# A grouped-query decode step with a gated MLP: 64 rows of an MLP weight in five groups, x in the result's layout by products, and nine scratch products per head

## The chip, the cores and the metric

The kernel runs on one core of a Trainium2 chip. The core has a matrix engine (TensorE, PE in the rows; PEld is its loading of the stationary operand), a vector engine (VectorE, DVE), a scalar engine (ScalarE, ACT), GpSimd (POOL) and SyncE (SP), which here only issues transfers. Sixteen DMA engines move data between HBM and the core's memory. The metric is the device time of one launch in microseconds (us), as a median over runs; lower is better.

## The reference, cut to what matters

One decode step for eight sequences of width 512, all in float32: a normalised x goes through attention over a cache of 4096 keys and values (32 query heads, 8 key/value heads of width 128), and through a gated MLP whose result, after a silu, multiplies the attention's result; x is added at the end.

```python
def _A_ref(x, k_cache, v_cache, wq, wo):
    q = (x @ wq).reshape(B, 1, 32, 128).transpose(0, 2, 1, 3)
    k, v = repeat(k_cache, 4, axis=1), repeat(v_cache, 4, axis=1)
    p = softmax(einsum("bhqd,bhkd->bhqk", q, k) * 128 ** -0.5)
    return einsum("bhqk,bhkd->bhqd", p, v).reshape(B, 1, 4096) @ wo

def _B_ref(x, w_in, w_sp, b_sp, w_out):
    z = gelu(x @ w_in)                         # 512 -> 1792
    z1, z2 = z[..., :896], layernorm(z[..., 896:])
    return (z1 * (w_sp * z2 + b_sp)) @ w_out   # 896 -> 512

xn = layernorm(x)
return x + _A_ref(xn, ...) * silu(_B_ref(xn, ...))
```

## The kernel before

**Data and slots.** The caches are 268 MB, and nearly all of the rest of the traffic is wq, wo and the MLP's weights. Three slots in the core's memory, a, b and c, take 8.39 MB each (128 partitions of 64 KB). A key/value head needs four slot loads: two halves of K (four sequences each) and two halves of V. SyncE issues all loads from one queue in a fixed order (`loads`): for each head the second half of K into b, the first half of V into c, the second half of V into b, and then the next head's first half of K into a. Before each it waits on a counter that TensorE raises (`pe`, eight steps a head), so that a load starts only when the slot's last reader is done; it stands one or two loads ahead of TensorE. After the last V come six pieces of wo into slot a (`WO_PIECES`, of 36, 16, 4, 4, 3 and 1 half-columns), and last x in the result's layout (`x_rows`, 128 rows of 256 bytes).

**The prologue** (`prologue`) runs under a scheduler that orders work by its dependencies. It loads wq into b, x (8 rows) and the MLP's weights (`w_mlp`, 128 rows) into c, and the first half of K into a. It normalises x, makes all q (L150), and when wq has been read, issues the next half of K into b (L160). Then it computes the MLP: z (L175), gelu, layernorm, the transposes to `hT` (L205), the product with `w_out` in seven blocks of 128 rows (L210, which writes four 32-row groups of one bank side by side), a re-layout by a selection matrix `pick` (L216) and the gate. Only then may slot c be loaded with V.

**A head** (`head_products` on TensorE, a hardware loop of eight turns, and `head_sides` on the other engines): 64 score products (L353), a softmax whose maxima and sums go across partitions by three small products (L357 to L361), the transpose of p, 32 products with each half of V (L372), and a fold of the output (L382), before whose second half two scratch products run (L379). Each take of a semaphore (`take`, L341) stands in TensorE's queue ahead of the products that need it. The second half of V is a separate wait.

**The end** (`last_products`, `last_sides`): for wo's rows of the first seven heads, 56 products in two accumulators (L408), which wait piece by piece; then the last head's rows directly (L417), the two accumulators copied out (one by VectorE, one by ScalarE) and folded in by `pick` (L430), and the last two rows of wo (L417 again). VectorE multiplies by the gate and adds x (both shown as L258), and ScalarE issues the store.

Of the kernel before, what the change touches and what calls it, by code (L numbers as in the profile page):

```python
# [10 lines left out]
P = 128  # L11
B, D = 8, 512
HKV, REP, S, DH = 8, 4, 4096, 128
NK = D // P
G = 4
J = S // (G * P)
R = 32
FH = 896
FQ = 256
NB = FH // P  # L20
# [5 lines left out]
W = 64  # L26
OUT_ROWS = 2 * B
# [1 line left out]
FOLDED = HKV * REP - REP  # L29
AHEAD = FOLDED + 2  # L30
HD = 256
N_IN, N_OUT = NK * 2 * FH, NB * D
N_MLP = N_IN + N_OUT + R
STEPS = 8
WARM = 384


class Chip:
# [49 lines left out]
        self.same_all = self.same.rearrange("p g r -> p (g r)")  # L88


def prologue(tc, t, x, w_mlp, wq, k0, k1, landed_a, landed_b):

    nc = tc.nc
    slot_a, slot_b, slot_c = t.slots
    nc.sync.dma_start(slot_b, wq)
    wq_sb = slot_b.rearrange("p (k n) -> p k n", k=NK)
    w_in_sb = slot_c[:, :N_IN].rearrange("p (k n) -> p k n", k=NK)
    w_out_sb = slot_c[:, N_IN:N_IN + N_OUT].rearrange("p (j d) -> p j d", j=NB)
    side_sb = slot_c[:, N_IN + N_OUT:N_MLP]
    x_sb = slot_c[:B, N_MLP + P:N_MLP + P + D]  # L100
    xn = slot_c[:B, N_MLP + P + D:N_MLP + P + 2 * D]
    nc.sync.dma_start(x_sb, x)
    nc.sync.dma_start(slot_c[:, :N_MLP], w_mlp)
    first = nc.sync.dma_start(slot_a, k0).then_inc(landed_a, 16)
    tc.no_tile_sem_insts.add(first.ins.name)

# [21 lines left out]
    def scratch(*shape):  # L128
        turn[0] ^= 1
        n = 1  # L130
        for s in shape[1:]:
            n *= s
        return t.scr[turn[0]][:shape[0], :n]
# [11 lines left out]
    for quad in range(HKV // G):  # L145
        pq = scratch(P, REP * DH)
        for k in range(NK):
            for g in range(G):
                lo = (quad * G + g) * REP * DH
                nc.tensor.matmul(pq[R * g:R * (g + 1), :], t.xnT[:, k, :], wq_sb[:, k, lo:lo + REP * DH],  # L150
                                 start=(k == 0), stop=(k == NK - 1))
# [12 lines left out]
    z, u_sb = zu[:, 0], zu[:, 1]  # L164
    rest = t.pT.rearrange("p j b g r -> p (j b g r)")
    hT, y_sb = rest[:, :2 * P].rearrange("p (a s) -> p a s", a=2), rest[:, D:]
# [36 lines left out]
    for a in range(2):  # L203
        th = scratch(P, P)
        nc.tensor.transpose(th, u_sb[:, 1, a * P:(a + 1) * P], t.ident)  # L205
        nc.vector.tensor_copy(hT[:, a, :], th)
    pw = scratch(P, D)
    for j in range(NB):
        g, a = divmod(j, 2)
        nc.tensor.matmul(pw[R * g:R * (g + 1), :], hT[:, a, R * g:R * (g + 1)], w_out_sb[:, j, :],  # L210
                         start=(a == 0), stop=(a == 1 or j == NB - 1))
    nc.vector.tensor_copy(y_sb, pw)
    py = scratch(P, W)
    for g in range(G):
# [6 lines left out]
    nc.vector.tensor_scalar(e, e, 1.0, None, op0=ALU.add)  # L221
    nc.vector.reciprocal(e, e)
    nc.vector.tensor_mul(t.gate, py, e)


def place_q(nc, t, h):
# [3 lines left out]
class Heads:  # L230
# [2 lines left out]

    def __init__(self, nc, t, landed_a, landed_b, stored):
        self.nc, self.t = nc, t
        self.pe, self.dve, self.act = (nc.alloc_semaphore(s) for s in ("pe", "dve", "act"))
        self.token, self.part1 = nc.alloc_semaphore("token"), nc.alloc_semaphore("part1")
        self.landed_a, self.landed_b, self.landed_c = landed_a, landed_b, nc.alloc_semaphore("landed_c")  # L240
        self.landed_wo = [nc.alloc_semaphore(f"landed_wo{i}") for i in range(len(WO_PIECES))]
        self.landed_x = nc.alloc_semaphore("landed_x")
        self.stored = stored
        self.nv = self.na = 0
        self.end = HKV * STEPS
        half_d = D // 2
        self.part = [t.sc[:, 0, :half_d], t.o_ps[0].rearrange("p g d -> p (g d)")[:, :half_d]]
# [13 lines left out]
    def tell(self):  # L261
        self.nc.vector.wait_ge(self.dve, self.nv).then_inc(self.token, 1)

    def loads(self, kT, v, wo, x_rows):
        sync, (a, b, c) = self.nc.sync, self.t.slots
        for h in range(HKV):
            at = h * STEPS
            if h:
                sync.wait_ge(self.pe, at - 8 + 7)
                sync.dma_start(b, kT[h, 1]).then_inc(self.landed_b, 16)  # L270
                sync.wait_ge(self.pe, at - 8 + 6)
            sync.dma_start(c, v[h, 0]).then_inc(self.landed_c, 16)
            sync.wait_ge(self.pe, at + 2)
            sync.dma_start(b, v[h, 1]).then_inc(self.landed_b, 16)
            sync.wait_ge(self.pe, at + 1)
            if h < HKV - 1:
                sync.dma_start(a, kT[h + 1, 0]).then_inc(self.landed_a, 16)
        for (lo, hi), landed in zip(WO_PIECES, self.landed_wo):
            sync.dma_start(a[:, lo * HD:hi * HD], wo[:, lo * HD:hi * HD]).then_inc(landed, 16)
        sync.dma_start(self.t.x_out, x_rows).then_inc(self.landed_x, 16)  # L280

    def head_sides(self, h):

# [41 lines left out]
    def last_sides(self, out):  # L325
        nc, t, vec = self.nc, self.t, self.nc.vector
        self.v(vec.tensor_copy, t.part_sb[0], self.part[0], pe=self.end + 1)
        self.tell()
        nc.scalar.wait_ge(self.pe, self.end + 2)
        nc.scalar.copy(t.part_sb[1], self.part[1]).then_inc(self.part1, 1)  # L330
        vec.wait_ge(self.act, self.na).then_inc(self.act, -self.na)
        self.v(vec.tensor_mul, t.gate, t.acc, t.gate, pe=self.end + 3)
        vec.wait_ge(self.landed_x, 16).then_inc(self.landed_x, -16)
        self.v(vec.tensor_add, t.gate, t.gate, t.x_out, own=True)
        nc.scalar.wait_ge(self.dve, self.nv)
        nc.scalar.dma_start(out, t.gate).then_inc(self.stored, 16)
        nc.scalar.wait_ge(self.dve, self.nv).then_inc(self.dve, -self.nv)
        vec.wait_ge(self.pe, self.end + 3).then_inc(self.pe, -(self.end + 3))
# [4 lines left out]
    def head_products(self):  # L343
        nc, t, step = self.nc, self.t, lambda mm: mm.then_inc(self.pe, 1)
        slot_a, slot_b, slot_c = t.slots
        for half, (slot, landed) in enumerate(((slot_a, self.landed_a), (slot_b, self.landed_b))):
            self.take(landed, 16)
            k_sb = slot.rearrange("p (i c g s) -> p i c g s", i=HALF, c=2, g=G)
            for i in range(HALF):
                b = half * HALF + i  # L350
                for c in range(2):
                    for g in range(G):
                        mm = nc.tensor.matmul(t.sc[R * g:R * (g + 1), c, :], t.q[:, b * R:(b + 1) * R],  # L353
                                              k_sb[:, i, c, g, :], start=(b == 0), stop=(b == B - 1))
            step(mm)
        self.take(self.token, 1)
        step(nc.tensor.transpose(t.scr[0][:1, :P], t.nm, t.ident))  # L357
        self.take(self.token, 1)
        step(nc.tensor.transpose(t.scr[1][:, :1], t.full.rearrange("b g r -> b (g r)"), t.ident[:1, :1]))
        self.take(self.token, 1)  # L360
        step(nc.tensor.matmul(t.scr[1][:, 1:2], t.same_all, t.wl, start=True, stop=True))  # L361
        self.take(self.token, 1)
        pT = t.pT.rearrange("p j b g r -> p j b (g r)")
        for half, (slot, landed) in enumerate(((slot_c, self.landed_c), (slot_b, self.landed_b))):
            if half:
                self.take(self.token, 1)
            self.take(landed, 16)
            v_sb = slot.rearrange("p (i j e) -> p i j e", i=HALF, j=J)
            of = t.o_ps[half].rearrange("p g d -> p (g d)")
            for j in range(J):  # L370
                for i in range(HALF):
                    mm = nc.tensor.matmul(of[R * i:R * i + G * REP, :], pT[:, j, half * HALF + i],  # L372
                                          v_sb[:, i, j], start=(j == 0), stop=(j == J - 1))
            step(mm)
        n = HALF * REP
        for half in range(2):
            if half:
                for _ in range(2):
                    nc.tensor.matmul(t.scr[1][:, :WARM], t.ident, pT.rearrange("p j b x -> p (j b x)")[:, :WARM],  # L379
                                     start=True, stop=True)  # L380
            self.take(self.token, 1)
            mm = nc.tensor.matmul(t.po[:, half * n:(half + 1) * n], t.o_sb[half],  # L382
                                  t.fold.rearrange("p i r -> p (i r)"), start=True, stop=True)
        step(mm)
# [53 lines left out]
        step(mm)  # L438


def gqa_gmlp_decode(nc, x, kT, v, wq, wo, w_mlp, x_rows, out):
    t = Chip(nc)
    landed_a, landed_b, stored = (nc.alloc_semaphore(s) for s in ("landed_a", "landed_b", "stored"))
    with tile.TileContext(nc) as tc:
        prologue(tc, t, x, w_mlp, wq, kT[0, 0], kT[0, 1], landed_a, landed_b)
    heads = Heads(nc, t, landed_a, landed_b, stored)
    heads.loads(kT, v, wo, x_rows)
    for h in range(HKV):
        heads.head_sides(h)
    heads.last_sides(out)  # L450
    nc.sync.wait_ge(stored, 16).then_inc(stored, -16)
    with nc.tensor.Fori(0, HKV):
        heads.head_products()
    heads.last_products()
# [39 lines left out]
```

## Time and profile before

| | |
|---|---|
| median of 3 runs | 678.75 us (678.70 to 679.01) |
| the profiled execution's own time | 679.39 us |
| its span, first to last instruction | 678.1 us |
| TensorE busy | 351.0 us (52%) |
| VectorE busy | 80.7 us (12%) |
| 16 DMA engines, SyncE's queue | 99.1% of the span |
| HBM read | 290.78 MB, 429 GB/s over the span |
| TensorE's granted clock, mean | 0.748 |

The page's second part cuts the span into 40 slices and gives each engine's busy share in tenths; its third part gives what each DMA queue moved. A timeline gives single instructions, or runs of the same, in order of time, with the idle time ahead of them in brackets and what ended it. "PEq" is TensorE's own queue: an instruction stood there for a semaphore. A DMA row gives the size and the time from issue to landing. The granted clock is given as a share of 2.4 GHz, so 0.50 is 1.2 GHz.

### The profile page before, as it was taken

The page shows a single profiled execution, that of the slowest core. Times are in us where ns is not written, and L with a number is a line of the kernel's source. Part 1 is how long each engine was busy: PE and PEld are TensorE (multiplying, and loading weights), DVE is VectorE, ACT ScalarE, POOL GpSimd, SP SyncE. Part 2 cuts the span into 40 slices and gives each one's busy share as a digit, 9 for nine tenths or more (in the row PEclk, how much of TensorE's full clock was granted, in tenths as well). Part 3 has the DMA queues.
Part 4 walks back from the last instruction along what each step waited for, and adds up shares of the span by engine and source line. Part 5 has one row for each costly group of instructions (what it writes and reads, how often), then busy time and mean ns, then how long its engine had stood idle before and what let it go on. Part 6 is the DMA issues. An engine that isn't in the chain of part 4 may idle for free. (4 is left out here: it accounts for less than half of the span.)

```text
span 678.1 us, 5431 instructions
## 1 busy us (share of the span) xinstructions
PE 351.0 (52%) x2480; PEld 102.7 (15%) x2480; DVE 80.7 (12%) x156; ACT 13.8 (2%) x28; POOL 2.8 (0%) x15
## 2 busy tenths in 40 slices
PE   0446743545565444456555444655645454655548
PEld 0112210111121111111111110111111111211104
DVE  0142021102110021101100021101101021100111
ACT  0010000000000000000000000000000000000000
POOL 1000000000000000000000000000000000000000
PEclk9986766778767677877766677887666678877659
DMA  9999999999999999999999999999999999999996
GB/s 383 439 433 434 434 433 433 434 433 433 433 433 433 433 433 433 437 437 437 445 437 433 437 437 433 441 437 433 433 433 433 433 433 433 433 433 433 433 414 287
DMA packets 6070, 290.90 MB, mean 429 GB/s; under 512 B 936, under 2 KB 1064, under 8 KB 1456
## 3 DMA queue, kind: packets, MB, share of 16 engines
q1 hardware_dynamic: 5920, 290.79, 99.1%
q8 instruction: 4, 0.07, 0.0%
q10 hardware_dynamic: 144, 0.03, 0.0%
q14 instruction: 2, 0.02, 0.0%
HBM read 290.78 MB, written 0.03 MB: 429 GB/s over the span
## 5 line engine op out<-in xcount | busy, mean ns | idle before, releaser
L372 PE MATMUL o_ps<-slot_b,pT 128*16 128x512 f32 x512 | 74.9, 751 | 81.0 <-PEq L341 81.0
L353 PE MATMUL sc<-slot_b,q 128*32 128x512 f32 x512 | 74.4, 746 | 73.5 <-PEq L341 73.5
L353 PE MATMUL sc<-slot_a,q 128*32 128x512 f32 x512 | 75.5, 756 | 56.2 <-PEq L341 56.2
L372 PE MATMUL o_ps<-slot_c,pT 128*16 128x512 f32 x512 | 73.9, 742 | 47.9 <-PEq L341 47.9
L258 DVE TENSOR_REDUCE nm<-sc 128x1 f32<-128x1024 f32 x8 | 9.8, 1225 | 277.0 <-PE sc L353 277.0
L258 DVE TENSOR_TENSOR o_all<-o_ps,diag 128x512 f32<-128x512 f32 x16 | 11.1, 692 | 243.4 <-PE o_ps L372 243.4
L353 PEld LDWEIGHTS sc<-slot_b,q 128*32 128x32 f32 x512 | 20.4, 134 | 127.5 <-issue 127.5
L372 PEld LDWEIGHTS o_ps<-slot_b,pT 128*16 128x16 f32 x512 | 17.6, 114 | 138.4 <-issue 138.4
L353 PEld LDWEIGHTS sc<-slot_a,q 128*32 128x32 f32 x512 | 20.7, 135 | 104.7 <-issue 104.7
L372 PEld LDWEIGHTS o_ps<-slot_c,pT 128*16 128x16 f32 x512 | 17.4, 114 | 97.7 <-issue 97.7
L289 ACT ACTIVATE p<-sc,nm 128x1024 f32<-128x1024 f32 x8 | 8.9, 1114 | 554.4 <-DVE nm L258 554.4
L258 DVE TENSOR_REDUCE o_sb<-o_all 128x128 f32<-128x512 f32 x16 | 16.4, 1025 | 0.5
L142 PE MATMUL scr<-ident,slot_c 8*128 8x8 f32 x4 | 0.6, 255 | 25.2 <-DVE slot_c L139 25.2
L379 PE MATMUL scr<-pT,ident 128*128 128x384 f32 x32 | 12.3, 507 | 0.0
L258 DVE STREAM_TRANSPOSE pT<-p 128x1024 f32<-128x1024 f32 x8 | 10.0, 1245 | 0.3
L150 PE MATMUL scr<-slot_b,xnT 128*32 128x512 f32 x64 | 9.0, 717 | 0.3 <-DVE xnT L143 0.3
L357 PE MATMUL scr<-ident,nm 128*1 128x128 f32 x8 | 2.2, 269 | 11.9 <-PEq L341 11.9
L382 PE MATMUL po<-fold,o_sb 128*128 128x16 f32 x32 | 6.1, 266 | 2.5 <-PEq L341 2.5
L361 PE MATMUL scr<-wl,same 128*128 128x1 f32 x16 | 3.6, 297 | 6.6 <-PEq L341 6.6
L382 PEld LDWEIGHTS po<-fold,o_sb 128*128 128x128 f32 x32 | 4.8, 188 | 14.0 <-issue 14.0
L258 DVE TENSOR_SCALAR p<-p,w,wl 128x1024 f32<-128x1024 f32 x8 | 6.5, 813 | 0.3
L379 PEld LDWEIGHTS scr<-pT,ident 128*128 128x128 f32 x32 | 5.5, 191 | 2.1
(92 smaller groups left out, 77.9 us busy)
## 6 DMA issues: line engine op xcount, KB each, us to landing
slot_c<-in_w_mlp SPq DMA_DIRECT2D x1, 5392.0 KB, 33.8
slot_a<-in_wo SPq DMA_DIRECT2D x1, 4608.0 KB, 40.1
slot_a<-in_wo SPq DMA_DIRECT2D x1, 2048.0 KB, 44.5
slot_a<-in_wo SPq DMA_DIRECT2D x2, 512.0 KB, 45.7
slot_a<-in_wo SPq DMA_DIRECT2D x1, 384.0 KB, 46.7
slot_a<-in_kT SPq DMA_DIRECT2D x8, 48.1
slot_b<-in_kT SPq DMA_DIRECT2D x8, 29.2
slot_c<-in_v SPq DMA_DIRECT2D x8, 48.1
```

What stands on the lines that cost most here:

```text
L142: nc.tensor.transpose(pt[:, k * B:(k + 1) * B], xn[:, k * P:(k + 1) * P], t.ident[:B, :B])
L150: nc.tensor.matmul(pq[R * g:R * (g + 1), :], t.xnT[:, k, :], wq_sb[:, k, lo:lo + REP * DH], start=(k == 0), stop=(k == NK - 1))
L258: make(*args, **kw).then_inc(self.dve, 1)
L289: nc.scalar.activation(p, t.sc.rearrange("p c s -> p (c s)"), AF.Exp, bias=t.nm, accum_out=t.l).then_inc(self.act, 1)
L353: mm = nc.tensor.matmul(t.sc[R * g:R * (g + 1), c, :], t.q[:, b * R:(b + 1) * R], k_sb[:, i, c, g, :], start=(b == 0), stop=(b == B - 1))
L357: step(nc.tensor.transpose(t.scr[0][:1, :P], t.nm, t.ident))
L361: step(nc.tensor.matmul(t.scr[1][:, 1:2], t.same_all, t.wl, start=True, stop=True))
L372: mm = nc.tensor.matmul(of[R * i:R * i + G * REP, :], pT[:, j, half * HALF + i], v_sb[:, i, j], start=(j == 0), stop=(j == J - 1))
L379: nc.tensor.matmul(t.scr[1][:, :WARM], t.ident, pT.rearrange("p j b x -> p (j b x)")[:, :WARM], start=True, stop=True)
L382: mm = nc.tensor.matmul(t.po[:, half * n:(half + 1) * n], t.o_sb[half], t.fold.rearrange("p i r -> p (i r)"), start=True, stop=True)
```

## The change

Four things change.

1. **w_out.** The last of its seven blocks of 128 rows is split. Its upper 64 rows no longer stand as whole rows in `w_mlp`; they lie there as 128 half rows, so that `w_mlp`'s rows become 1 KB shorter. Its lower 64 rows (with one row of zeros, 65 in all) come by a transfer of their own, `w_lane`, of five groups of 13 rows of 2 KB; in HBM there is an unused row behind each group, so the groups don't join. The seventh block's product becomes three: one over the lower 64 rows, and one for each half of the columns over the half rows, for which `h_half` holds the upper part of the hidden vector in the partitions that fit, zeros elsewhere.
2. **x_rows** and its wait are gone. `x_out` is made in the prologue: eight products of `pick` with x as it was loaded, and a copy.
3. **Nine scratch products** of 128x512 run in each head between the first and the second half of V, in a hardware loop inside the loop over heads, ahead of the waits for the second half.
4. SyncE's order: `w_lane` stands between `w_mlp` and the first half of K, and nothing stands behind the last piece of wo.

SyncE's queue in the prologue before; `in_kT` is K, `in_w_mlp` the MLP's weights:

```order
L95 DMA slot_b<-in_wq 128x16384
L102 DMA slot_c<-in_x 8x512
L103 DMA slot_c<-in_w_mlp 128x10784
L104 DMA slot_a<-in_kT 128x16384
L160 DMA slot_b<-in_kT 128x16384
```

The same queue now:

```order
L98 DMA slot_b<-in_wq 128x16384
L106 DMA slot_c<-in_x 8x512
L107 DMA slot_c<-in_w_mlp 128x10528
L111 DMA slot_c<-in_w_lane 65x1x512
L112 DMA slot_a<-in_kT 128x16384
L168 DMA slot_b<-in_kT 128x16384
```

`w_mlp`'s rows are 256 elements shorter, and one more transfer stands ahead of the first K.

TensorE's queue in a head, from the last small product of the softmax to the fold, before (`scr` is scratch, `o_ps` the attention's output):

```order
L361 MATMUL scr<-wl,same 128x1
L372 MATMUL o_ps<-slot_c,pT 16x512 x32
L372 MATMUL o_ps<-slot_b,pT 16x512 x32
L382 MATMUL po<-fold,o_sb 128x16
L379 MATMUL scr<-pT,ident 128x384 x2
L382 MATMUL po<-fold,o_sb 128x16
```

The same stretch now:

```order
L384 MATMUL scr<-wl,same 128x1
L398 MATMUL o_ps<-slot_c,pT 16x512 x32
L390 UNCONDITIONAL_BRANCH
L391 MATMUL scr<-pT,ident 128x512
L390 REGISTER_ALU
L390 COMPARE_AND_BRANCH
L398 MATMUL o_ps<-slot_b,pT 16x512 x32
L408 MATMUL po<-fold,o_sb 128x16
L405 MATMUL scr<-pT,ident 128x384 x2
L408 MATMUL po<-fold,o_sb 128x16
```

The loop's one product is executed nine times, with a register operation and a branch behind each.

TensorE's queue at the end of the prologue before:

```order
L189 MATMUL scr<-part_sum,same 128x1 x2
L205 MATMUL scr<-ident,p 128x128 x2
L210 MATMUL scr<-slot_c,pT 32x512 x7
L216 MATMUL scr<-pT,pick 32x64 x8
```

And now:

```order
L197 MATMUL scr<-part_sum,same 128x1 x2
L213 MATMUL scr<-ident,p 128x128 x2
L217 MATMUL scr<-ident,p 64x32
L224 MATMUL scr<-slot_c,pT 32x512 x6
L227 MATMUL scr<-slot_c,pT 32x512
L229 MATMUL scr<-slot_c 32x256 x2
L234 MATMUL scr<-pT,pick 32x64 x8
L245 MATMUL scr<-slot_c,pick 32x64 x8
```

One small transpose, two products of the split block and eight for x have been added.

The diff, without the host's import of sizes:

```diff
--- before.py
+++ after.py
@@ -29,10 +29,13 @@
 FOLDED = HKV * REP - REP
 AHEAD = FOLDED + 2
 HD = 256
-N_IN, N_OUT = NK * 2 * FH, NB * D
+WHOLE = NB - 1
+LANES, ROWS = 5, 13
+N_IN, N_OUT = NK * 2 * FH, WHOLE * D + D // 2
 N_MLP = N_IN + N_OUT + R
 STEPS = 8
 WARM = 384
+AHEAD_OF_V = 9
 
 
 class Chip:
@@ -88,19 +91,24 @@
         self.same_all = self.same.rearrange("p g r -> p (g r)")
 
 
-def prologue(tc, t, x, w_mlp, wq, k0, k1, landed_a, landed_b):
+def prologue(tc, t, x, w_mlp, w_lane, wq, k0, k1, landed_a, landed_b):
 
     nc = tc.nc
     slot_a, slot_b, slot_c = t.slots
     nc.sync.dma_start(slot_b, wq)
     wq_sb = slot_b.rearrange("p (k n) -> p k n", k=NK)
     w_in_sb = slot_c[:, :N_IN].rearrange("p (k n) -> p k n", k=NK)
-    w_out_sb = slot_c[:, N_IN:N_IN + N_OUT].rearrange("p (j d) -> p j d", j=NB)
+    w_out_sb = slot_c[:, N_IN:N_IN + WHOLE * D].rearrange("p (j d) -> p j d", j=WHOLE)
+    w_half_sb = slot_c[:, N_IN + WHOLE * D:N_IN + N_OUT]
     side_sb = slot_c[:, N_IN + N_OUT:N_MLP]
     x_sb = slot_c[:B, N_MLP + P:N_MLP + P + D]
     xn = slot_c[:B, N_MLP + P + D:N_MLP + P + 2 * D]
     nc.sync.dma_start(x_sb, x)
     nc.sync.dma_start(slot_c[:, :N_MLP], w_mlp)
+    spare = N_MLP + P + 2 * D
+    w_lane_sb = slot_c[:LANES * ROWS, spare:spare + D]
+    h_half = slot_c[:, spare + D:spare + D + 2 * R].rearrange("p (e s) -> p e s", e=2)
+    nc.sync.dma_start(w_lane_sb, w_lane[:, :ROWS])
     first = nc.sync.dma_start(slot_a, k0).then_inc(landed_a, 16)
     tc.no_tile_sem_insts.add(first.ins.name)
 
@@ -204,11 +212,21 @@
         th = scratch(P, P)
         nc.tensor.transpose(th, u_sb[:, 1, a * P:(a + 1) * P], t.ident)
         nc.vector.tensor_copy(hT[:, a, :], th)
+    last_rows, low, high = slice((G - 1) * R, P), slice(0, P // 2), slice(P // 2, P)
+    tl = scratch(P // 2, R)
+    nc.tensor.transpose(tl, u_sb[last_rows, 1, P // 2:P], t.ident[last_rows, last_rows])
+    nc.vector.memset(h_half, 0.0)
+    nc.vector.tensor_copy(h_half[low, 0], tl)
+    nc.vector.tensor_copy(h_half[high, 1], hT[high, 0, last_rows])
     pw = scratch(P, D)
-    for j in range(NB):
+    for j in range(WHOLE):
         g, a = divmod(j, 2)
         nc.tensor.matmul(pw[R * g:R * (g + 1), :], hT[:, a, R * g:R * (g + 1)], w_out_sb[:, j, :],
-                         start=(a == 0), stop=(a == 1 or j == NB - 1))
+                         start=(a == 0), stop=(a == 1))
+    pl = pw[last_rows, :]
+    nc.tensor.matmul(pl, hT[low, 0, last_rows], w_lane_sb[low, :], start=True, stop=False)
+    for e in range(2):
+        nc.tensor.matmul(pl[:, e * (D // 2):(e + 1) * (D // 2)], h_half[:, e], w_half_sb, start=False, stop=(e == 1))
     nc.vector.tensor_copy(y_sb, pw)
     py = scratch(P, W)
     for g in range(G):
@@ -221,6 +239,12 @@
     nc.vector.tensor_scalar(e, e, 1.0, None, op0=ALU.add)
     nc.vector.reciprocal(e, e)
     nc.vector.tensor_mul(t.gate, py, e)
+    px = scratch(P, W)
+    for g in range(G):
+        for a in range(2):
+            nc.tensor.matmul(px[R * g:R * (g + 1), :], t.pick[:B, a, :],
+                             x_sb[:, (2 * g + a) * W:(2 * g + a + 1) * W], start=(a == 0), stop=(a == 1))
+    nc.vector.tensor_copy(t.x_out, px)
 
 
 def place_q(nc, t, h):
@@ -239,7 +265,6 @@
         self.token, self.part1 = nc.alloc_semaphore("token"), nc.alloc_semaphore("part1")
         self.landed_a, self.landed_b, self.landed_c = landed_a, landed_b, nc.alloc_semaphore("landed_c")
         self.landed_wo = [nc.alloc_semaphore(f"landed_wo{i}") for i in range(len(WO_PIECES))]
-        self.landed_x = nc.alloc_semaphore("landed_x")
         self.stored = stored
         self.nv = self.na = 0
         self.end = HKV * STEPS
@@ -261,7 +286,7 @@
     def tell(self):
         self.nc.vector.wait_ge(self.dve, self.nv).then_inc(self.token, 1)
 
-    def loads(self, kT, v, wo, x_rows):
+    def loads(self, kT, v, wo):
         sync, (a, b, c) = self.nc.sync, self.t.slots
         for h in range(HKV):
             at = h * STEPS
@@ -277,7 +302,6 @@
                 sync.dma_start(a, kT[h + 1, 0]).then_inc(self.landed_a, 16)
         for (lo, hi), landed in zip(WO_PIECES, self.landed_wo):
             sync.dma_start(a[:, lo * HD:hi * HD], wo[:, lo * HD:hi * HD]).then_inc(landed, 16)
-        sync.dma_start(self.t.x_out, x_rows).then_inc(self.landed_x, 16)
 
     def head_sides(self, h):
 
@@ -330,7 +354,6 @@
         nc.scalar.copy(t.part_sb[1], self.part[1]).then_inc(self.part1, 1)
         vec.wait_ge(self.act, self.na).then_inc(self.act, -self.na)
         self.v(vec.tensor_mul, t.gate, t.acc, t.gate, pe=self.end + 3)
-        vec.wait_ge(self.landed_x, 16).then_inc(self.landed_x, -16)
         self.v(vec.tensor_add, t.gate, t.gate, t.x_out, own=True)
         nc.scalar.wait_ge(self.dve, self.nv)
         nc.scalar.dma_start(out, t.gate).then_inc(self.stored, 16)
@@ -363,6 +386,9 @@
         pT = t.pT.rearrange("p j b g r -> p j b (g r)")
         for half, (slot, landed) in enumerate(((slot_c, self.landed_c), (slot_b, self.landed_b))):
             if half:
+                flat = t.pT.rearrange("p j b g r -> p (j b g r)")
+                with nc.tensor.Fori(0, AHEAD_OF_V):
+                    nc.tensor.matmul(t.scr[1], t.ident, flat[:, :512], start=True, stop=True)
                 self.take(self.token, 1)
             self.take(landed, 16)
             v_sb = slot.rearrange("p (i j e) -> p i j e", i=HALF, j=J)
@@ -438,13 +464,13 @@
         step(mm)
 
 
-def gqa_gmlp_decode(nc, x, kT, v, wq, wo, w_mlp, x_rows, out):
+def gqa_gmlp_decode(nc, x, kT, v, wq, wo, w_mlp, w_lane, out):
     t = Chip(nc)
     landed_a, landed_b, stored = (nc.alloc_semaphore(s) for s in ("landed_a", "landed_b", "stored"))
     with tile.TileContext(nc) as tc:
-        prologue(tc, t, x, w_mlp, wq, kT[0, 0], kT[0, 1], landed_a, landed_b)
+        prologue(tc, t, x, w_mlp, w_lane, wq, kT[0, 0], kT[0, 1], landed_a, landed_b)
     heads = Heads(nc, t, landed_a, landed_b, stored)
-    heads.loads(kT, v, wo, x_rows)
+    heads.loads(kT, v, wo)
     for h in range(HKV):
         heads.head_sides(h)
     heads.last_sides(out)
@@ -461,8 +487,6 @@
 
     c = np.ascontiguousarray
     x = c(A_x).reshape(B, D)
-    x_rows = np.zeros((G, R, W), np.float32)
-    x_rows[:, :OUT_ROWS] = x.reshape(B, G, 2, W).transpose(1, 2, 0, 3).reshape(G, OUT_ROWS, W)
     side = np.zeros((P, R), np.float32)
     side[:, 0] = c(B_w_sp).reshape(())
     side[:, 1] = c(B_b_sp).reshape(())
@@ -471,6 +495,9 @@
     k = c(A_k_cache).reshape(2, HALF, HKV, G, R, 2, J * G // 2, DH)
     vv = c(A_v_cache).reshape(2, HALF, HKV, P, J, G, DH)
     w_out = c(B_w_out).reshape(NB, P, D)
+    w_lane = np.zeros((LANES * ROWS, D), np.float32)
+    w_lane[:P // 2] = w_out[-1, :P // 2]
+    w_lane = np.pad(w_lane.reshape(LANES, ROWS, D), ((0, 0), (0, 1), (0, 0)))
     arrays = {
         "x": x,
         "kT": c(k.transpose(2, 0, 7, 1, 5, 3, 6, 4)).reshape(HKV, 2, P, SLOT),
@@ -479,9 +506,10 @@
         "wo": c(w_o.transpose(1, 0, 2)).reshape(P, SLOT),
         "w_mlp": np.concatenate([
             c(B_w_in).reshape(NK, P, 2 * FH).transpose(1, 0, 2).reshape(P, NK * 2 * FH),
-            w_out.transpose(1, 0, 2).reshape(P, NB * D),
+            w_out[:-1].transpose(1, 0, 2).reshape(P, WHOLE * D),
+            w_out[-1, P // 2:].reshape(P // 2, 2, D // 2).transpose(1, 0, 2).reshape(P, D // 2),
             side], axis=1),
-        "x_rows": x_rows.reshape(P, W),
+        "w_lane": w_lane,
```

## Rows read from the trace of the kernel before

**Rows 1.** The page, DMA queues: packets, MB, share of 16 engines.

```profile
q1 hardware_dynamic: 5920, 290.79, 99.1%
q8 instruction: 4, 0.07, 0.0%
q14 instruction: 2, 0.02, 0.0%
```

**Rows 2.** Timeline of SyncE's last issues: start us, us, instruction.

```profile
625.53 0.33 SPq L274 DMA_DIRECT2D slot_b<-in_v  x1
...
625.90 2.80 SPq L279 DMA_DIRECT2D slot_a<-in_wo  x6
...
628.75 0.43 SPq L280 DMA_DIRECT2D x_out<-in_x_rows  x1
```

**Rows 3.** DMA issues: size each, us from issue to landing.

```profile
slot_a<-in_wo SPq DMA_DIRECT2D x1, 4608.0 KB, 40.1
...
slot_a<-in_wo SPq DMA_DIRECT2D x1, 384.0 KB, 46.7
...
slot_a<-in_wo SPq DMA_DIRECT2D x1, 128.0 KB, 46.4
x_out<-in_x_rows SPq DMA_DIRECT2D x1, 32.0 KB, 46.1
```

**Rows 4.** Timeline from the last half of V to the store.

```profile
655.32 9.91 PE L372 MATMUL o_ps<-slot_b,pT 128*16 128x512 f32 x64 [9.98 <-PEq L341]
...
665.41 1.54 PE L379 MATMUL scr<-pT,ident 128*128 128x384 f32 x4
...
667.64 0.62 PE L408 MATMUL sc<-slot_a,oT 128*8 128x256 f32 x8
...
674.39 0.37 ACT L330 COPY part_sb<-o_ps 128x256 f32<-128x256 f32 x1 [45.76 <-PE o_ps L408]
...
675.12 0.42 PE L430 MATMUL acc<-part_sb,pick 128*16 128x64 f32 x16 [0.38 <-PEq L341]
...
675.34 0.64 PE L417 MATMUL acc<-slot_a,oT_last 128*16 128x64 f32 x32
676.04 0.23 DVE L258 TENSOR_TENSOR gate<-acc,gate 128x64 f32<-128x64 f32 x1 [1.28 <-PE acc L417]
676.30 0.23 DVE L258 TENSOR_TENSOR gate<-gate,x_out 128x64 f32<-128x64 f32 x1
```

**Rows 5.** Stretches with second halves of V: PE and PEld busy, granted clock, DMA.

```profile
268.00:278.00 10.00, 8.72 (x64) 2.08 (x64) 0.80 1.00 433
...
423.00:434.00 11.00, 9.94 (x64) 2.27 (x64) 0.73 1.04 453
...
655.00:666.00 11.00, 9.91 (x64) 2.28 (x64) 0.72 0.96 416
```

**Rows 6.** Stretches between the last two V halves: five engines, granted clock, DMA.

```profile
647.00:648.00 1.00, 0.00 (x0) 0.00 (x0) 0.15 (x1) 0.00 (x0) 0.00 (x0) 0.73 0.76 328
...
649.00:655.00 6.00, 0.00 (x0) 0.00 (x0) 0.00 (x0) 0.00 (x0) 0.00 (x0) 0.50 0.90 390
```

**Rows 7.** Stretches of the last transfers; the last two columns are DMA share and GB/s.

```profile
671.00:672.00 1.00, 1.00 (x28) 0.52 (x22) 0.00 (x0) 0.00 (x0) 0.00 (x0) 1.00 1.03 419
...
673.00:673.50 0.50, 0.50 (x14) 0.25 (x10) 0.00 (x0) 0.00 (x0) 0.00 (x0) 1.00 0.32 113
673.50:674.00 0.50, 0.50 (x16) 0.30 (x10) 0.00 (x0) 0.00 (x0) 0.00 (x0) 1.00 0.29 90
```

**Rows 8.** Timeline of TensorE, the prologue's end and the first head's scores.

```profile
58.42 0.45 PE L216 MATMUL scr<-pT,pick 128*32 128x64 f32 x16 [0.92 <-DVE pT L212]
61.53 9.86 PE L353 MATMUL sc<-slot_a,q 128*32 128x512 f32 x64 [2.65 <-PEq L341]
75.41 9.75 PE L353 MATMUL sc<-slot_b,q 128*32 128x512 f32 x64 [4.02 <-PEq L341]
```

**Rows 9.** Timeline of SyncE, its first issue after the prologue.

```profile
61.25 0.33 SPq L272 DMA_DIRECT2D slot_c<-in_v  x1
```

## The prediction

> **What bounds the kernel now.** I read the queues first: SyncE's queue keeps the sixteen DMA engines occupied for 99.1% of the span [rows 1]. With 290.8 MB to bring, a change inside the body is worth something only if it takes bytes from the engine that ends last, or if it makes the queue run dry. So I then read the end, in SyncE's timeline, the landing times and TensorE's timeline.
>
> The last half of V is issued at 625.53 and TensorE starts on it at 655.32, after waiting 9.98 us [rows 2, 4]. From there TensorE is without a gap until 674.3: 9.91 us of V products, then the fold, then 56 products with wo from 667.64. Two copies follow, the fold of the accumulators from 675.12, and the last products, which end at 675.98. The multiplication, the addition and the store take the rest of the span.
>
> The pieces of wo land beside this. The first was issued at 625.90 and landed 40.1 us later, at 666.0; six issues take 2.80 us, so the fifth starts near 627.8 and lands at 674.5, and the sixth near 628.3 and lands at 674.7 [rows 2, 3]. In this execution the last piece was there about 0.4 us before the fold of the accumulators began. So TensorE ended last, and the transfers stood only a little ahead of it.
>
> The profiled execution took 679.39 us, 1.3 us more than its span; the median of the runs is 678.75, 0.64 less. The rows give a reason. The V products of a second half took 8.72, 9.94 and 9.91 us in three heads, and the mean granted clock beside them was 0.80, 0.73 and 0.72 [rows 5]. The profiled execution drew nearly the longest form in its last head. A run that draws a shorter one meets the last piece of wo instead of TensorE.
>
> **The change part by part.**
>
> *Nine scratch products.* They fill TensorE's wait ahead of the second half of V, so that its clock is still at 2.4 GHz when that half lands. First what it can give. In the stretch from 655 to 666 the mean clock was 0.72 over 11 us, so 2 x 0.28 x 11 = 6.2 us were at 1.2 GHz, 0.3 of them before the products began; the 5.8 us of work would take 2.9 us at full clock. The half then takes 7.0 us. The same sum on the 268 to 278 stretch (products from 268.6) gives 8.72 - 1.7 = 7.0 as well [rows 5].
>
> Then what they cost. At full clock 32 V products, four side by side in the array, take 7.0 us, so one group of four streams its 512 columns in 0.87 us; a product over all columns of the array streams as many. From above: two 384-column scratch products take 1.54 us with their filling [rows 4], 0.77 each, or 1.03 for 512 columns. Nine take 7.8 to 9.2 us. TensorE has 9.98, so they end 0.7 to 2.1 us before the half lands. After the last product before that wait, at 645.34, the clock was full until about 647.5, that is 2.1 us (0.73 is its mean from 647 to 648), and 0.50 from there to 655 [rows 6]. So a gap of this size should mostly keep the clock. I take the whole 2.9 us.
>
> What is late next? The wo products would be ready at 664.7, but the first piece lands at 666.0. From there 6.65 us of products end near 672.7, so TensorE reaches the fifth piece before it is there, at 674.5. Of the 32 records behind the fold, 24 need that piece and 8 the last: 0.64 us, with 0.1 to wake, gives 675.25 in place of 675.98. This term is -0.7 in the profiled execution: 678.7. That is what the fastest shown runs already take, so against the median it is worth almost nothing.
>
> In the other seven heads a faster half only frees slot b sooner, for a queue that never runs dry.
>
> *The 64 rows of w_out.* w_mlp's rows lose 1 KB, so each of sixteen engines loses 8 rows of 1 KB, 8.2 KB. One engine moves 433/16 = 27 GB/s [rows 5], so this is -0.30 us on each. The new transfer of 65 rows of 2 KB, on five engines, gives each of these 13 rows, 26.6 KB or 0.98 us: net +0.68 us on five and -0.30 on eleven. All of w_mlp lands long before it is used, so only the sum of an engine's bytes counts, and this carries through to the last piece of wo, since the queue never stops.
>
> The engines are not even now. From 671 to 672 the share is full (1.03); from 673.0 to 674.0 it is 0.32 and 0.29 [rows 7], and 5/16 is 0.31. Five engines end 1.3 to 1.5 us after the other eleven. If these five are not the ones that carry the new rows, the last landing is 0.30 us earlier, and the loaded ones still end before it (1.3 - 0.68 - 0.30). If one of them is, it is up to 0.68 later. The trace does not number engines; five of sixteen drawn blind make either likely enough, and I take -0.30 as the nearer, since only the engine that ends last among the five decides, and it is spared in 11 of 16 cases. Bounds: -0.30 and +0.68.
>
> A rule of the Trainium skill speaks against such a transfer (DMA: Bandwidth & Descriptors, "Rules for kernel authors"): a small outermost dimension confines a transfer to that many engines. By that rule the five groups are what puts the rows on five engines, and +0.68 is its price; no row of the trace shows a transfer of such a shape.
>
> *x_rows.* It landed at 628.75 + 46.1 = 674.85 [rows 2, 3], behind the last piece; the addition that needs it starts at 676.30 [rows 4]. In the DMA-bound case the addition would start near 675.5, still later. Its removal gives 0, at most 0.1 from freeing the engines.
>
> *The prologue.* Added are a small transpose, two products net, eight products for x, two or three small copies and a memset. The nearest rows are the eight `pick` products, 0.45 us with 0.92 of waiting ahead [rows 8]; two such hand-overs and a transpose are 2 to 3 us; a gain is excluded, since nothing is taken from the prologue's chain but one product. They move the first V issue from 61.25 [rows 9] to about 64. What hides this: the transfer queued ahead of it is K's second half, whose products start only at 75.41 after 4.02 us of waiting [rows 8], so the queue has work for about 11 us after the prologue's end. Without that cover they would cost their 2 to 3 us. SyncE gains one issue, which no later instruction waits for, and loses one at its end.
>
> The sum: 679.39 - 0.7 - 0.3 = 678.4 us, with 0 for x and the prologue. Against the median, 678.75, it is -0.35 us (0.05%). A measurement of this kernel tells about 0.2%, or 1.36 us, from no change.
>
> **The rivals.**
>
> *The late engines are among the loaded five.* For it: sixteen engines, five late, five loaded. Against it: the last alone decides. The end of the transfers is 0.68 later and not 0.30 earlier: 678.7 + 0.7 = 679.4.
>
> *The clock falls in the remaining gap.* For it: the gap's upper end, 2.1 us, is just how long the clock held [rows 6]. Then the last half takes 8.7 to 9.9 us as before, and the kernel lies between the DMA's end and the present times: 678.5 to 678.8.
>
> *The transfer does not do what it says.* If its 65 rows spread over sixteen engines, each gets back its 8.2 KB and nothing shifts: 678.7.
>
> *The late engines come level: faster.* The other work on the engines is six instruction loads, 0.07 and 0.02 MB [rows 1], each some 10 to 17 KB, 0.4 to 0.6 us of one engine; five late engines and six such loads fit. If the changed code moves them to other engines or past the end, all pieces land up to 1.3 us sooner: 678.4 - 1.3 = 677.1, where TensorE's chain (679.39 - 2.9 = 676.5) still allows it. Against it: the code is almost the same length, so the loads should stay.
>
> *The scratch loop's turn is dear: slower.* Each product is followed by a register operation and a branch, and no row shows what a short loop's turn costs on TensorE. It lies ahead of the last half's wait. With t for a turn, the nine end at 9 x (0.87 to 1.03 + t); beyond 9.98 us the half starts late. The 2.9 us from the clock pay for some of it, so the chain is longer than the profile's from 9t = 3.6 to 5.0, and beyond 0.2% over the median from about t = 0.5 to 0.63 us. At t = 1 us it is 679.4 + 4 to 5.4, some 684. Against it: the loop over heads has the same two instructions, and q8 shows four loads of instructions in all [rows 1], not one for each turn. The Trainium skill (Runtime: NRT & Kernel Launch, "Instruction fetch mechanics") says that a taken branch stalls when its target lies outside the pages at hand; here the target is one product back, so by that rule t is small, and the four loads agree.
>
> **How the numbers follow.** Forecast 678.4: 0.42. Late engines loaded, 679.4: 0.22. Clock falls, 678.5 to 678.8: 0.18. No shift, 678.7: 0.04. Engines level, 677.1: 0.07. Dear loop, 680.1 and more: 0.07. The bounds of the transfer (-0.30 to +0.68), about 0.5 below for part of the fourth rival, and 0.1 for the wake give 677.6 to 679.5, which leaves out the last two. Faster by over 0.2% is the level case, 0.07; slower the dear loop, 0.07; within 0.2% the rest, 0.86.
>
> **What would show it.** The last V half should take about 7 us at a granted clock near 1.00; the wo products should begin when the first piece lands and wait for pieces after it; the last stretch with a share near 0.3 should end 0.3 us earlier, or the sharing engines be other than five. The nine products should take 7.8 to 9.2 us in each head and end before the half lands. I am wrong if the V half starts later than its landing, if it is still at 1.2 GHz, or if the DMA share drops below full anywhere in the body.

## The result and the profile after: slower, at the transfers' end

The changed kernel takes 681.59 us in the median of 22 runs (679.97 to 776.43), the kernel before 678.97 in the same series (678.37 to 679.73). The ratio is 1.0043, 95% interval 1.0031 to 1.0055: slower. Five of the 22 runs, of 757 to 776 us, are left out of the ratio; elsewhere such a time came twice, both with a transfer in groups (757.39 us with the split of w_out alone, 756.58 with two groups), and never in the kernel before. Of the other 17, ten lie between 679.97 and 680.63 and the rest go up to 687.99; their mean is 681.87, their median 680.61. The profiled execution took 680.61 us, so its trace speaks of the usual run, some 1.6 us over the median of before. Its span is 679.0 us, with 1.6 us around it.

First the part that went as intended. TensorE's timeline of the changed kernel, from the scratch products to those behind the second piece of wo; the bracket is the wait ahead, where it was long, and what ended it:

```profile
646.84 7.99 PE L391 MATMUL scr<-pT,ident 128*128 128x512 f32 x18
...
656.98 7.06 PE L398 MATMUL o_ps<-slot_b,pT 128*16 128x512 f32 x64 [2.15 <-PEq L364]
...
667.84 0.62 PE L434 MATMUL sc<-slot_a,oT 128*8 128x256 f32 x8 [1.42 <-PEq L364]
...
672.71 0.64 PE L434 MATMUL sc<-slot_a,oT 128*8 128x256 f32 x8 [0.38 <-PEq L364]
```

Nine products (18 records) take 7.99 us and leave a gap of 2.15; the last half of V takes 7.06 us where it took 9.91 [rows 4]. Then TensorE waits for the first piece of wo, and once more, 0.38 us, for a later one: it is now ahead of the transfers. The stretches of two second halves of V, with the granted clock in the third column from the end:

```profile
423.00:434.00 11.00, 9.14 (x72) 3.20 (x72) 1.92 (x3) 0.00 (x0) 0.00 (x0) 1.00 1.02 441
...
655.00:666.00 11.00, 8.77 (x70) 2.89 (x70) 1.73 (x2) 0.00 (x0) 0.00 (x0) 1.00 0.96 416
```

The clock is 1.00 where it was 0.73 and 0.72 [rows 5]; it holds over a gap of 2.15 us.

Now the end, from the copy of the accumulators on:

```profile
675.17 0.37 ACT L354 COPY part_sb<-o_ps 128x256 f32<-128x256 f32 x1 [44.98 <-PE o_ps L434]
675.90 0.54 PE L456 MATMUL acc<-part_sb,pick 128*16 128x64 f32 x16
676.27 0.64 PE L443 MATMUL acc<-slot_a,oT_last 128*16 128x64 f32 x32
676.97 0.23 DVE L283 TENSOR_TENSOR gate<-acc,gate 128x64 f32<-128x64 f32 x1 [1.43 <-PE acc L443]
```

The last products end at 676.91, before at 675.98 [rows 4]. They start 0.26 us after the last row of wo is written (676.01 and 676.27); before, this took 0.99 us (674.35 and 675.34). These are the stretches of the last transfers (the last two columns are the DMA share and GB/s):

```profile
671.00:672.00 1.00, 1.00 (x20) 0.41 (x8) 0.00 (x0) 0.00 (x0) 0.00 (x0) 1.00 1.05 422
673.00:673.50 0.50, 0.50 (x16) 0.26 (x10) 0.00 (x0) 0.00 (x0) 0.00 (x0) 1.00 0.59 233
673.50:674.00 0.50, 0.50 (x17) 0.27 (x11) 0.00 (x0) 0.00 (x0) 0.00 (x0) 1.00 0.52 195
...
674.50:675.00 0.50, 0.50 (x12) 0.07 (x4) 0.00 (x0) 0.00 (x0) 0.00 (x0) 1.00 0.08 31
675.00:675.50 0.50, 0.40 (x28) 0.36 (x28) 0.39 (x1) 0.33 (x1) 0.00 (x0) 1.00 0.06 25
675.50:676.00 0.50, 0.41 (x31) 0.27 (x22) 0.04 (x1) 0.04 (x1) 0.00 (x0) 1.00 0.06 23
```

One engine of sixteen is 0.06 of the share. From 674.5 on, one engine works almost alone until the last row is written at 676.01; before, the share was 0.32 and 0.29 from 673 to 674 [rows 7], and the last row was written at 674.35. So the last piece is 1.67 us later. The queues of the two kernels differ by no instruction load:

```profile
q1 hardware_dynamic: 5846, 290.76, 99.1%
q8 instruction: 4, 0.07, 0.0%
q14 instruction: 2, 0.02, 0.0%
```

The bytes are as good as the same [rows 1]; it is how they stand on the engines that differs.

To split the 1.67 us I took the records of single packets. They do not name engines, but on one engine a 64 KB row follows the last, so each row's start can be joined to the end of one before it, which gives sixteen series. For the last row of the last V half I read when the first of the sixteen engines starts it, how far the latest is behind, and when the last row of wo is written (one execution each):

| kernel | first engine | latest behind it | last row written |
|---|---|---|---|
| before | 650.38 | 2.01 | 674.35 |
| changed | 650.73 | 3.33 | 676.01 |
| split of w_out alone, 5 groups | 650.62 | 3.03 | 675.60 |
| split in 8 groups | 650.59 | 2.82 | 675.36 |
| split in 64 single rows | 650.77 | 1.99 | 674.72 |
| unused rows, 5 groups | 650.90 | 3.13 | 675.98 |
| unused rows, 4 groups | 650.80 | 2.95 | 675.70 |
| unused rows, 2 groups | 651.61 | 2.15 | 675.72 |
| unused rows, 5 groups of long rows | 651.25 | 2.78 | 675.99 |
| split, groups issued first | 651.19 | 2.54 | 675.69 |
| changed without the split | 650.45 | 1.80 | 674.20 |

Of the 1.67 us, 0.35 is on all engines and 1.32 on the one that ends last. Five kernels have no groups (the one before, the changed one without the split, and three with one part each, below): there the first engine starts at 650.38 to 650.92 and the latest is 1.65 to 2.01 behind, so only the second part is clear of what such traces differ by. The first part shows nearer its cause: the second row of K begins at 37.30 in the changed kernel and at 36.87 to 37.01 in those five.

The series also say which engine ends last (each has the same 256 rows of K and V, and a load of instructions stands in the gap between two rows of one series). In the changed kernel five engines start their first row of K at 35.66 to 36.34, behind the groups, and the other eleven at 34.24 to 34.83 (before, all sixteen at 34.54 to 35.01). One of the five also carries both loads of q14, at 92.0 and 559.0, and it is the one that ends last: it starts its last V row at 654.06, the other four at 651.90 to 652.25. Before, too, the engine with both loads of q14 ended last. Its second row of K starts at 37.30 there and at 38.92 in the changed kernel, so 1.62 of the 1.67 us are lost by then.

### The profile page after: what moved, and what is told of

It is laid out like the page before. It is cut to its first block, busy times and chain, and to the rows that moved or that the text cites. A ratio compares the mean times of both kernels' runs of the same rounds, so it can differ in the third digit from the quotient of the medians.

```text
span 679.0 us, 5917 instructions
## 1 busy us (share of the span) xinstructions
PE 398.2 (59%) x2645; PEld 128.0 (19%) x2645; DVE 81.5 (12%) x160; ACT 13.8 (2%) x28; POOL 2.8 (0%) x15
## 5 line engine op out<-in xcount | busy, mean ns | idle before, releaser
L376 PE MATMUL sc<-slot_b,q 128*32 128x512 f32 x512 | 70.8, 715 | 72.7 <-PEq L364 72.7
L376 PE MATMUL sc<-slot_a,q 128*32 128x512 f32 x512 | 73.9, 742 | 66.4 <-PEq L364 66.4
L398 PE MATMUL o_ps<-slot_b,pT 128*16 128x512 f32 x512 | 61.6, 636 | 18.2 <-PEq L364 18.2
L391 PE MATMUL scr<-pT,ident 128*128 128x512 f32 x144 | 63.9, 598 | 0.0
L391 PEld LDWEIGHTS scr<-pT,ident 128*128 128x128 f32 x144 | 26.7, 190 | 37.4 <-issue 37.4
```

The costliest lines, as they stand in the source:

```text
L391: nc.tensor.matmul(t.scr[1], t.ident, flat[:, :512], start=True, stop=True)
```

## The experiments

Times are medians of all runs, with the kernel before in the same series behind them, and the ratio with its interval. The edits are cut to their main lines.

**The parts one by one.** Three theories stood: the transfer in five groups costs the time ("groups"); the short loop on TensorE does ("loop"); the removed load of x does. The first kernel has the split of w_out alone, x loaded as before and no scratch products:

```diff
+LANES, ROWS = 5, 13
-N_IN, N_OUT = NK * 2 * FH, NB * D
+N_IN, N_OUT = NK * 2 * FH, WHOLE * D + D // 2
+    nc.sync.dma_start(w_lane_sb, w_lane[:, :ROWS])
```

> Only the 64 rows of w_out come in five groups; x_rows is loaded as before and there are no scratch products ahead of the second V half. Theory 'groups' (the 2 KB rows take far longer on their five engines than their bytes, and the first K rows beside them are slowed): the last piece of wo lands 1.0 to 1.7 us later, 679.8 to 680.6 us, and no wide spread. Theory 'loop' (the scratch loop's turns cost the time): no change against the kernel before, 678.7 to 679.2, since no loop is here.

Measured: 680.32 us against 678.81, ratio 1.0026 [1.0015, 1.0037]. The split alone makes the usual run as slow as the whole change, and the end has the same shape:

```profile
674.50:675.00 0.50, 0.50 (x24) 0.28 (x22) 0.04 (x1) 0.00 (x0) 0.00 (x0) 1.00 0.07 26
675.00:675.50 0.50, 0.39 (x29) 0.22 (x16) 0.38 (x1) 0.37 (x1) 0.00 (x0) 1.00 0.07 25
675.50:676.00 0.50, 0.16 (x12) 0.19 (x16) 0.00 (x0) 0.00 (x0) 0.00 (x0) 1.00 0.03 8
```

The next two are the kernel before with the nine products, in a loop, and written out (`for _ in range(AHEAD_OF_V)`):

```diff
+                with nc.tensor.Fori(0, AHEAD_OF_V):
+                    nc.tensor.matmul(t.scr[1], t.ident, flat[:, :512], start=True, stop=True)
```

> Only the nine scratch products, in their hardware loop; w_out and x_rows as before. Theory 'groups': the last V half at full clock, the end set by the last piece of wo, 678.4 to 678.8 us, and a narrow spread. Theory 'loop': single executions several us longer, 681 to 688, as in the changed kernel, with the median at 679.5 or more.

> Only the nine scratch products, written out nine times instead of looped; w_out and x_rows as before. Both theories: 678.4 to 678.8 us. If this spreads like the changed kernel too, the products themselves are to blame and not the loop.

Measured: 678.74 and 678.98 against 678.81, ratios 1.0002 [0.9994, 1.0011] and 1.0004 [0.9995, 1.0013]. The loop theory falls: looped and written out cost the same, and neither cost can be told from none. The products also bring nothing, though the last V half is nearly 3 us shorter.

The fourth has x by products alone:

```diff
-        sync.dma_start(self.t.x_out, x_rows).then_inc(self.landed_x, 16)
+            nc.tensor.matmul(px[R * g:R * (g + 1), :], t.pick[:B, a, :],
+                             x_sb[:, (2 * g + a) * W:(2 * g + a + 1) * W], start=(a == 0), stop=(a == 1))
```

> Only x by products and no x_rows load. Both theories: nothing behind the last piece of wo was waited for, so 678.7 to 679.0 us, the same as the kernel before within 0.2%.

Measured: 678.86 against 678.81, 1.0002 [0.9994, 1.0011]: no change that can be told.

**Is it the five groups?** The same split, with the same bytes, in 64 groups of one row, and in 8 of eight:

```diff
-LANES, ROWS = 5, 13
+LANES, ROWS = 64, 1
```

> As e1 (only the split of w_out; x_rows loaded, no scratch products), but the same 64 rows of 2 KB come in 64 groups of one row, so that they go to all sixteen engines, four rows each. Theory 'five engines' (the cost is that five engines carry 13 rows each and end late): no engine is favoured, 678.8 to 679.1 us, the same as the kernel before. Theory 'any 2 KB rows' (rows of this size beside the stream of K slow everything, wherever they go): part or all of e1's 1.4 us stays, 679.4 to 680.3.

```diff
-LANES, ROWS = 5, 13
+LANES, ROWS = 8, 8
```

> As e1, but the 64 rows come in eight groups of eight rows. Theory 'five engines', by the bytes: eight engines get 16.4 KB and lose 8.2 KB, +0.3 us, so 679.1 us; by the time that a row took in e1 (about 0.13 us), 1.04 - 0.30 = +0.7 us, so 679.5. In both the cost lies between e5 and e1.

Measured: 679.36 and 679.72 against 678.90, ratios 1.0006 [0.9996, 1.0016] and 1.0008 [0.9998, 1.0018]. Neither can be told from no change, but the order of the medians, 64, 8, 5 groups, is that of the lags in the table (1.99, 2.82, 3.03). With 64 groups no engine works alone for long at the end (this execution, of 678.92 us, is the fastest of its kernel):

```profile
674.00:674.50 0.50, 0.50 (x32) 0.34 (x25) 0.24 (x1) 0.25 (x1) 0.00 (x0) 1.00 0.28 88
674.50:675.00 0.50, 0.42 (x32) 0.43 (x32) 0.00 (x0) 0.00 (x0) 0.00 (x0) 1.00 0.05 14
675.00:675.50 0.50, 0.50 (x35) 0.33 (x22) 0.00 (x0) 0.00 (x0) 0.00 (x0) 1.00 0.00 0
```

The first row of K still takes 2.51 to 2.89 us in it, 2.42 before, so the short rows slow the stream a little on all engines too.

**Bytes, rows or engines?** The next two leave w_out whole and add to the kernel before a transfer of zeros that nothing uses: 65 rows of 2 KB in five groups, or ten rows of 13 KB, the same bytes in as many groups.

```diff
+    nc.sync.dma_start(slot_c[:65, spare:spare + 512], extra[:, :13])
```

> The kernel before, with an unused transfer added behind w_mlp: five groups of 13 rows of 2 KB into spare columns of slot c; nothing else is changed. Theory 'bytes' (an engine ends later by what its bytes take): +0.98 us on five engines, so 679.8 if the latest engine is one of them, 678.8 to 679.2 if not. Theory 'rows' (13 short rows take more than their bytes): +1.4 to +2.0, so 680.2 to 680.8.

```diff
+    nc.sync.dma_start(slot_c[:10, spare:spare + 3328], extra[:, :2])
```

> As e7, with as many bytes in ten rows: five groups of two rows of 13 KB. Theory 'bytes': the same time as e7. Theory 'rows': less than e7, 679.5 to 679.9 us, since 26 KB then take 0.98 us on an engine.

Measured: 680.56 against 678.90, 1.0034 [1.0012, 1.0056], and 680.84, 1.0026 [1.0014, 1.0037]. The transfer alone is enough; the split of the product plays no part. The theory that many short rows are dear falls: ten long ones cost as much. Yet it isn't the bytes at the stream's rate either. By bytes 13 rows take 0.98 us of an engine; their records take 1.48 us in the mean of the five engines. These are two stretches of the changed kernel's packets around the groups:

```profile
DMA packets 67, 0.80 MB, mean 803 GB/s; under 512 B 16, under 2 KB 16, under 8 KB 56
```

```profile
DMA packets 35, 0.38 MB, mean 316 GB/s; under 512 B 5, under 2 KB 5, under 8 KB 30
```

The 2 KB rows are those under 8 KB and not under 2 KB: 40 start from 34.2 to 35.2 and 25 from 35.2 to 36.4, so 25 of 65 start where by bytes the groups would be ending. Of these rows of 2 KB the 24 quickest take 0.084 us, as do the eight such rows of x, which come by themselves; the other 41 take 0.10 to 0.17. Of the ten long rows five take 0.50 to 0.55 us and the other five 0.89 to 1.01. And the first rows of K suffer on all sixteen engines: in the changed kernel they take 3.01 to 3.09 us on the eleven engines without a group and 2.58 to 2.92 behind the groups, 2.42 before. In the split alone and in both of these kernels, as in the changed one, the engine with the loads of q14 is one of the five that start K late.

**All parts but the split.**

```diff
-    w_half_sb = slot_c[:, N_IN + WHOLE * D:N_IN + N_OUT]
-    nc.sync.dma_start(w_lane_sb, w_lane[:, :ROWS])
+    w_out_sb = slot_c[:, N_IN:N_IN + N_OUT].rearrange("p (j d) -> p j d", j=NB)
```

> The changed kernel without the split of w_out: x by products, no x_rows load, and the nine scratch products in their loop. If the transfer in groups is the whole of the loss, 678.5 to 678.8 us, the same as the kernel before or 0.3 us less; if the parts only lose together, 679.3 or more.

Measured: 678.96 against 678.82, 1.0007 [0.9998, 1.0016]. Its TensorE takes the last half in 7.06 us and is done by 675.20, but the median doesn't move:

```profile
655.16 7.06 PE L379 MATMUL o_ps<-slot_b,pT 128*16 128x512 f32 x64 [1.47 <-PEq L345]
...
666.04 0.62 PE L415 MATMUL sc<-slot_a,oT 128*8 128x256 f32 x8 [1.43 <-PEq L345]
...
674.34 0.86 PE L424 MATMUL acc<-slot_a,oT_last 128*16 128x64 f32 x32
```

**Which engines?** If one of the loaded five was the last already, there must be a number of groups at which the lag jumps. The unused transfer in two and in four groups:

```diff
+    nc.sync.dma_start(slot_c[:26, spare:spare + 512], extra[:, :13])
```

> As e7 (an unused transfer in groups of 13 rows of 2 KB behind w_mlp), with two groups. Theory 'the latest engine is among the five' (one engine, which already ended last for two code loads of the 8 KB kind, also carries a group): a step, either all of e7's 1.7 us (680.3 to 680.6) if it is one of these two, or 678.9 to 679.3 if it is not. Theory 'contention alone' (each group costs something): about two fifths of e7's, 679.6.

```diff
+    nc.sync.dma_start(slot_c[:52, spare:spare + 512], extra[:, :13])
```

> As e10, with four groups. Theory 'the latest engine is among the five': 680.2 to 680.6 if it is one of these four, 679.0 to 679.4 if it is the fifth. Theory 'contention alone': about four fifths of e7's, 680.2, so that this run tells only together with e10.

Measured: 679.59 and 680.33 against 678.82, ratios 1.0008 [0.9999, 1.0018] and 1.0025 [1.0014, 1.0035]. The latest engine's lag is 2.15 with two groups, about as before, and 2.95 with four. The joined series agree: with two groups two engines start K late and neither has a load of q14; with four groups four do, and one of them has both. If the groups go to the engines in a fixed order, which no run shows, it takes the third or the fourth. With two groups all engines are late: in the one profile the stream itself is slow for some rounds, here the stretch of two K rows beside the same of before:

```profile
37.20:42.80 5.60, 3.92 (x35) 1.12 (x33) 2.06 (x5) 0.00 (x0) 0.00 (x0) 1.00 1.00 374
```

```profile
36.90:41.70 4.80, 4.29 (x36) 1.50 (x36) 1.15 (x4) 0.00 (x0) 0.00 (x0) 1.00 1.01 437
```

All engines are busy in both, at 374 and 437 GB/s; behind the first row of K a row takes 2.73 to 2.82 us for two rounds and 2.46 to 2.89 for a third, then 2.42 again. This execution took 679.91 us, among the longer of its kernel, so not every run need have these rounds; rows over 2.46 us on many engines at once occur without groups as well, by 0.1 us each (with the looped scratch products, at 120 to 180 us).

**Does the place in the queue matter?** The split alone, with its transfer issued ahead of wq, where no stream of long rows runs yet:

```diff
+    nc.sync.dma_start(w_lane_sb, w_lane[:, :ROWS])
     nc.sync.dma_start(slot_b, wq)
```

> As e1, with the grouped transfer issued first of all, ahead of wq, and not between w_mlp and K. Theory 'beside the stream' (rows in five groups take twice their time, and slow the others, when they run beside rows of K): 13 rows at 0.084 us are 1.1 us, less 0.3, and no common delay, so 679.5 us. Theory 'bytes on the latest engine': the place in the queue doesn't matter, 680.2 to 680.4 as in e1.

Measured: 680.64 against 678.82, 1.0028 [1.0019, 1.0037]: as dear as behind w_mlp. Its first rows of K take 2.42 us, but the first row of wq starts 1.0 us later (2.74, before 1.74). The expected gain from a quiet place did not come; the price moved from one form into the other.

None of the twelve kernels is shown to be faster than the one before.

## Why the prediction was wrong

**The nine scratch products** went by the working: 7.99 us (7.8 to 9.2 expected), a gap of 2.15 (0.7 to 2.1, so just outside), the V half 7.06 (7.0), the clock kept, the wo products waiting for their pieces. The kernels with these products alone also bear out that this is worth nothing in the median, since the transfers end there.

**x_rows and the prologue** are worth nothing, as written. The cover named for the prologue held: V's first issue is at 64.39 now, 3.1 us later than [rows 9], and the products of K's second half still wait:

```profile
64.39 0.33 SPq L297 DMA_DIRECT2D slot_c<-in_v  x1
```

```profile
76.03 8.48 PE L376 MATMUL sc<-slot_b,q 128*32 128x512 f32 x64 [2.56 <-PEq L364]
```

**The dear loop turn** was the rival on the slower side; the looped and the written-out products refute it, since a turn costs nothing visible. That the kernel came out slower does not speak for it: the mechanism is another. The code loads stayed four and two, as the prediction held, and the level engines went with that. Its reading of the late engines was right: six loads, two of them on one engine, make five. Only their price was too low, 0.4 to 0.6 us; in the joined series a load of 8 KB puts its engine back by about 0.8 us and one of 16 KB by 1.3 to 1.5.

**The 64 rows of w_out** is the step that failed, twice.

First in its choice. It took -0.30 us "since only the engine that ends last among the five decides, and it is spared in 11 of 16 cases". A draw is no reading of a row, and the rival "the late engines are among the loaded five" is what happened: the engine that ends last is one of the five that start K late. The records of before, joined as above, would have told more than the draw: the engine that ends last there is put back about 0.8 us at 97.7 us and again at 559.8, as the two loads of q14 run, and nothing later gives this back. So why one engine ends last could be read. Whether five groups would take it could not: no row of before shows that, and this half stayed a draw. The rule of the Trainium skill that the prediction weighed (DMA: Bandwidth & Descriptors, "Rules for kernel authors"), that a small outermost dimension confines a transfer to that many engines, is borne out by the joined series: with five, four and two groups just five, four and two engines start K late.

Then in its bounds. Both were worked out from bytes at the stream's rate. The last row of wo is 1.67 us later in place of +0.68. The rows in groups ran at about two thirds of the stream's rate (1.48 us where their bytes take 0.98), and the first rows of K took 0.6 us longer on the eleven engines without a group. So these, too, are some 0.3 us late, where the prediction gave them 0.30 back: even with the late engine spared, -0.30 would not have come. The bounds would have had to allow for such rates; the trace of before has no transfer of that shape beside a stream, and I let the bytes stand. So even the rival's 679.4 was short of the usual 680.0 to 680.6.

With the measured 1.67 us in place of -0.30, the step's own sum would be 678.4 + 1.97 = 680.4 us, close to the usual run (680.61 is the median of the 17).

The rest of the ratio comes from single executions of 681 to 688 us. They are not explained, and none was traced. Elsewhere executions of 682 to 691 us came only with a transfer in groups (the unused rows in five and in two groups, and the groups issued first), and none in the kernel before.

Open, and not tried: where the rows in groups contend with the stream; in what order groups go to the engines; and what makes the long executions.

## What to carry to other kernels

A load that keeps sixteen queues full ends with its slowest engine: before an engine gets bytes of its own, find from the packet records which one is last and why, rather than counting chances. A small transfer in five groups beside such a stream cost 1.7 to 2.0 times what its bytes take, the delay of the stream itself included: the last row came 1.63 us later with the unused rows, and 1.97 us with the split once the 0.30 saved in w_mlp is put back, for 0.98 us of bytes. And an engine made faster under an end that the transfers set, as TensorE here by 2.9 us, is worth nothing.

## What was not expected of the hardware

The same bytes on five engines cost the same in rows of 2 KB and of 13 KB (680.56 and 680.84 us). Ahead of the stream they cost as much as inside it (680.64). In one trace the whole stream ran at 374 in place of 437 GB/s behind two small groups, with every engine counted as busy. And loads of instructions, of 8 or 16 KB, put the DMA engine that carries them back by 0.8 to 1.5 us, which stays to the end: that is why the engines of the kernel before do not end together.
